# One 512-column output projection for two token blocks of a first MLP, in place of two of 256 columns

## The chip, the core and the metric

The kernel runs on one core of a Trainium2 chip. The metric is the device time of one execution in microseconds (us); of the kernel before there are three runs. The core has a matrix engine (TensorE, PE in the rows; its weight loads are PEld), a vector engine (VectorE, DVE), an engine for functions (ScalarE, ACT), a general one (GpSimd, POOL) and one that issues transfers (SyncE, SP). Each runs its own instruction stream in order, and semaphores hold it back until the data it needs are there. TensorE writes its sums into PSUM, which has eight banks of 512 float32 numbers per partition; all else lies in SBUF.

## What is computed

```python
def reference(q, k, v, moe_*, moe2_*):
    # 4 sequences, 8 heads, 576 tokens, head size 64; causal window of 64 keys
    scores = where(0 <= i - j < 64, q @ k.T / 8, -1e9)
    attn = softmax(scores) @ v
    x = attn.transpose(0, 2, 1, 3).reshape(2304, 512)
    x = (sigmoid(x @ w_gate) * (x @ w_val)) @ w_out      # 512 -> 1536 -> 512
    return ((x @ w_a) * (x @ w_b)) @ w_out2              # 512 -> 1536 -> 512
```

The weights reach the core as 64-bit floats, so each matrix is decoded on the chip to float32 and split into a pair (h, l) of float32r tiles that sum to it. Data are split likewise, and a product is three matmuls: h·h, h·l, l·h.

## The kernel before

The 2304 tokens are nine blocks of 256 (`N`). `HALVES` puts blocks 0 to 4 into a first half and 5 to 8 into a second; in each half blocks are grouped: (0), (1, 2), (3, 4), then (5, 6), (7, 8). A half runs the first MLP (phase 0) for its blocks and then the second (phase 1). The hidden dimension is 12 chunks of 128; a *turn* of the plan takes one group and one to three chunks. In a first MLP the turns with the first three chunks take one block each; all later turns of a two-block group take both blocks at once.

For each chunk of a turn `hidden` makes two products over the model dimension (`gps` and `vps`, lines 301 and 303, 12 matmuls each on line 293, 512 columns for two blocks and 256 for one), each in one PSUM bank of `ps_gv` (three banks). ScalarE and VectorE make of them the hidden pair `hh`, `hl` (lines 307 to 318), from a pool of five. The output projection of a turn isn't made at once: each block's job goes into `queue` and is put out in the next turn, spread over that turn's chunks (line 479). A job `projection` takes two banks of `ps_acc` (which has two), runs over the turn's chunks, the four 128-row chunks of the output and the three products (line 332, 256 columns), and then `evacuate` adds both banks to the block's sums `xacc` in SBUF (line 351 on VectorE; line 349 on ScalarE for a block's first turn). After a block's last chunk the sums are rounded to `xh` (line 356, ScalarE) and the rest goes to `xl` (line 357, GpSimd): the input of the second MLP.

Between the products, `decode` prepares the weights, one matrix at a time: ScalarE (line 259), VectorE (262, 266, 269), GpSimd (272), VectorE (274, the float step), ScalarE (279, the rounding to `wah`, `wbh` or `woh`) and GpSimd (280, the rest `wal`, `wbl`, `wol`). There are four places for a chunk's weights, so a chunk waits for the readers of the chunk four before it. What `tile` schedules as each engine's order is fixed when the program is built.

Of the kernel before, what the change touches and what calls it, by code (L numbers as in the profile page):

```python
# [19 lines left out]
def tile_window_attention_gated_mlps(ctx, tc, q, k, v, w1g, w1v, w1o, w2a, w2b, w2o, out):  # L20
# [5 lines left out]
    NP = H // 2            # head pairs = chunks of the model dimension  # L26
    NF = DFF // P          # chunks of the hidden dimension
    G = 3                  # hidden chunks whose products are summed in PSUM
    N = 256                # tokens of a block
    TB = N // P            # 128-token tiles of a block  # L30
    # blocks that share their products over the model dimension, in two halves
    HALVES = (((0,), (1, 2), (3, 4)), ((5, 6), (7, 8)))
    W = 2 * N
    LAG = 1                # steps between the starts of two units of attention
    WIN = 64
    KW = P + WIN           # keys that a 128-query tile can see
    QSCALE = -1.0 / float(D) ** 0.5    # scores are kept negated
# [20 lines left out]
    # the tensor engine's clock is up by the time that the first rows are here  # L58
# [3 lines left out]
    # queries in halves of 64, each with its window of 128 keys; the rows are those of two heads.  # L62
    # key c of the window, WIN - c tokens before the half's first query, is open to query p for
    # p + 1 <= c <= p + WIN
# [13 lines left out]
    # the first half of a sequence has no keys before it  # L78
# [3 lines left out]
    # ---------------------------------------------------------------- attention  # L82
# [3 lines left out]
    # columns: pair of heads, half of the queries, head of the pair, query; Q of the even heads  # L86
    # above zeros, of the odd heads below zeros
# [13 lines left out]
    def attention(t, hq, xhi, xlo, c0):  # L101
        """Tokens [128 t, 128 t + 128) of heads [4 hq, 4 hq + 4); the result, split, goes to columns
        c0... of xhi, xlo. A generator: it stops where other work may come between."""
# [9 lines left out]
        # keys' window of the transposed K, two heads to a column; scores are kept negated  # L113
        # the first units have the banks to themselves
# [18 lines left out]
        # V of the 64 keys before the tile and of its first half  # L133
# [57 lines left out]
    # places of x: the result of the first MLP follows its input, and each group of the second  # L191
    # half one of the first half
# [3 lines left out]
    def new_x(phase, group):  # L196
        """Tiles for x of a group, in parts that sum to it; blocks have their slices."""
        w = len(group) * N
        place = PLACE[group]
        x[phase, group] = pair = tuple(  # L200
            xs.tile([P, NP, w], F32R, tag=f"x{p}{place}", name=f"x{p}{phase}_{group[0]}") for p in "hl"
        )
        for i, b in enumerate(group):
            x[phase, (b,)] = tuple(t[:, :, i * N:(i + 1) * N] for t in pair)

# [9 lines left out]
    def attention_stream(blocks):  # L215
        """The units of the blocks, a new one under way every LAG steps."""
# [15 lines left out]
    # ------------------------------------------------------------------ weights  # L232
    mats = ((w1g, w1v, w1o), (w2a, w2b, w2o))
    words = [[w.bitcast(I32) for w in m] for m in mats]    # float64: low word, high word
# [16 lines left out]
    def decode(F):  # L251
        """Hidden chunk's weights: float64 words to float32 (rounded at the 24th bit) and on to
        float32r pairs that sum to it exactly. A generator, one matrix at a time."""
        got = {}
        for nm in "abo":
# [4 lines left out]
            # the exponent: what lies below float32's range becomes 0  # L260
# [24 lines left out]
    # --------------------------------------------------------------------- MLPs  # L285
    def product(ps, w, x):
        """ps = w^T x over the model dimension; the product of the two rests is below what the
        sums keep."""
# [9 lines left out]
    def hidden(phase, w, x):  # L298
# [6 lines left out]
        if phase == 0:  # L305
            # the logistic function is (1 + tanh(x / 2)) / 2; tanh is in one table set with exp
# [14 lines left out]
    def project(phase, acc, w, h, begin, end):  # L321
# [7 lines left out]
        for m, ps in enumerate(outs):  # L329
            for n, (a, b) in enumerate(pairs):  # L330
                # a start clears the written bits of the whole bank: one for both of its sums
# [8 lines left out]
    def evacuate(phase, blk, acc, begin, end):  # L340
        """Adds the products of a few hidden chunks to what the block has so far."""
# [20 lines left out]
    # The turns of a phase: a block and the hidden chunks it takes. They are staggered, so that  # L362
    # chunks are done with, and others are needed, one at a time.
    # the first turns, and before each what is to be ready: blocks of attention, chunks of weights
# [9 lines left out]
    def turns(order, half, ph):  # L374
# [11 lines left out]
        if (half, ph) == (0, 0):     # as blocks come in one by one  # L386
# [29 lines left out]
    def step_decode(turn):  # L416
        """One matrix of the next chunk, if the place for it is free in this turn."""
# [24 lines left out]
    def attend(blk=None, steps=0):  # L442
        """Puts out attention up to the end of a block, or so many steps of it."""
# [5 lines left out]
    def projection(ph, blk, work, begin, end):  # L449
# [3 lines left out]
        evacuate(ph, blk, acc, begin, end)  # L453

    queue, begun = [], 0
    for n, (half, ph, group, fcs) in enumerate(plan):
# [14 lines left out]
        for i, fc in enumerate(fcs):  # L471
# [3 lines left out]
            if (half, ph) == (0, 1) and fc == NF - 1 and PLACE[group] == PLACE[HALVES[1][1]]:  # L475
                # the last reader of this place's x is out
                attend(HALVES[1][0][-1])
                feed = attention_stream(HALVES[1][1])
            for _ in range(-(-len(queue) // (len(fcs) - i))):
                projection(*queue.pop(0))  # L480
            for _ in group:
                step_decode(n)
                attend(steps=rate)
        for j, b in enumerate(group):
            sl = slice(j * N, (j + 1) * N)
            queue.append((ph, b, [(w, (hh[:, sl], hl[:, sl])) for w, (hh, hl) in hs], begin, end))
# [32 lines left out]
```

## Time and profile before

| | |
|---|---|
| median of three runs | 1041.39 us (1040.54 to 1041.55) |
| span of the profiled execution (its own time isn't listed beside it) | 1039.7 us |
| TensorE busy | 1007.7 us, 97% |
| VectorE, ScalarE, GpSimd busy | 74%, 45%, 43% |
| DMA engines, mean share | 32% |

Busy time counts a matmul from its start to its end, and matmuls overlap; what one costs is read from the distance of the starts. A wait is put down to what the profile saw end last, which need not be what the instruction waited for. "Granted clock" is the share of TensorE's full clock that it was given: 1.00 is 2.4 GHz, 0.50 is 1.2 GHz.

### The profile page before, as it was taken

The numbers are of one execution on the slowest core, as the hardware profiler recorded it, in microseconds if no ns is written. First come the engines' busy times: TensorE is split into PE (matmuls) and PEld (weight loads), VectorE is DVE, ScalarE is ACT, GpSimd is POOL, SyncE is SP. The second block draws the span as 40 slices with busy tenths as digits, with TensorE's granted clock in tenths as the row PEclk, the third lists the DMA queues.
The fourth block names the chain that finished last, engine by engine and source line by source line (L and its number), as shares of the span: only waits on it lengthen the run. The fifth ranks groups of instructions, "written<-read, shape, count | busy, mean of one in ns | idle before, by whom it ended". The sixth has DMA issues, their size and how long they took to land.

```text
span 1039.7 us, 16966 instructions
## 1 busy us (share of the span) xinstructions
PE 1007.7 (97%) x6278; PEld 886.0 (85%) x6278; DVE 766.4 (74%) x1414; ACT 467.7 (45%) x1075; POOL 447.9 (43%) x353
## 2 busy tenths in 40 slices
PE   7799999999999999999999999999999799999998
PEld 6799998989899788888888898988888788888886
DVE  5998378767868956856767696468787877787853
ACT  7887543332334665433423566333333444333320
POOL 2554055434527713524434242245454675454520
PEclk9999999999999999999999999999999999999999
DMA  8866233212312323323312372123232323232302
GB/s 203 202 174 159 57 112 102 82 61 81 102 45 78 97 76 102 102 61 102 102 61 81 100 215 63 42 81 99 84 102 81 102 74 103 86 103 82 102 1 81
DMA packets 122930, 99.92 MB, mean 96 GB/s; under 512 B 60896, under 2 KB 114400, under 8 KB 122848
## 3 DMA queue, kind: packets, MB, share of 16 engines
q1 hardware_dynamic: 122848, 98.85, 32.4%
q8 instruction: 49, 0.80, 0.3%
q14 instruction: 33, 0.27, 0.1%
HBM read 89.65 MB, written 4.72 MB: 91 GB/s over the span
## 4 chain that ended last, share of the span: by engine, by line
PE 63%; DVE 19%; POOL 7%; ACT 6%; issue 4%; DMA 1%; SPq 0%; DVEq 0%; POOLq 0%; ACTq 0%
PE acc L332 20%; PE vps L293 19%; PE gps L293 19%; DVE ex L262 5%; DVE ex L274 3%; DVE wi L269 3%; DVE xacc L351 2%; POOL wi L272 2%; POOL wal L280 2%; PE sps L146 2%; DVE hl L316 2%; POOL wol L280 1%; POOL wbl L280 1%; PE xps L182 1%; DVE wi L266 1%
## 5 line engine op out<-in xcount | busy, mean ns | idle before, releaser
L272 POOL TENSOR_TENSOR wi<-wi,low 128x512 int32<-128x512 int32 x144 | 196.6, 1365 | 107.1 <-DVE wi L269 84.0
L293 PE MATMUL gps<-xh,wah 128*128 128x512 f32 (+1 forms) x528 | 188.3, 357 | 1.9 <-ACT wah L279 1.9
L293 PE MATMUL vps<-xh,wbh 128*128 128x512 f32 (+1 forms) x528 | 186.0, 352 | 1.7 <-ACT hr L307 0.9
L293 PE MATMUL gps<-xh,wal 128*128 128x512 f32 (+1 forms) x528 | 186.0, 352 | 0.0
L293 PE MATMUL gps<-xl,wah 128*128 128x512 f32 (+1 forms) x528 | 186.0, 352 | 0.0
L293 PE MATMUL vps<-xh,wbl 128*128 128x512 f32 (+1 forms) x528 | 185.7, 352 | 0.0
L293 PE MATMUL vps<-xl,wbh 128*128 128x512 f32 (+1 forms) x528 | 185.3, 351 | 0.0
L280 POOL TENSOR_TENSOR wol<-ex,woh 128x512 fp32r<-128x512 f32 x48 | 67.1, 1397 | 179.9 <-ACT woh L279 179.9
L315 ACT ACTIVATE hh<-hr 128x512 fp32r<-128x512 f32 (+1 forms) x132 | 73.0, 553 | 150.6 <-DVE hr L311 77.4
L280 POOL TENSOR_TENSOR wal<-ex,wah 128x512 fp32r<-128x512 f32 x48 | 71.5, 1490 | 143.8 <-ACT wah L279 126.1
L332 PE MATMUL acc<-hh,woh 128*128 128x256 f32 x432 | 123.6, 287 | 5.5 <-ACT woh L279 5.3
L332 PE MATMUL acc<-hl,woh 128*128 128x256 f32 x432 | 123.7, 287 | 0.6 <-DVE hl L316 0.6
L332 PE MATMUL acc<-hh,wol 128*128 128x256 f32 x432 | 123.4, 286 | 0.0
L274 DVE SCALAR_TENSOR_TENSOR ex<-ex,wi 128x512 f32<-128x512 int32 x144 | 102.8, 714 | 16.2 <-POOL wi L272 11.2
L293 PEld LDWEIGHTS vps<-xh,wbh 128*128 128x128 f32 x528 | 100.0, 189 | 15.7 <-ACT hr L307 1.3
L280 POOL TENSOR_TENSOR wbl<-ex,wbh 128x512 fp32r<-128x512 f32 x48 | 73.0, 1520 | 92.3 <-ACT wbh L279 89.0
L293 PEld LDWEIGHTS gps<-xh,wah 128*128 128x128 f32 x528 | 100.2, 190 | 14.5 <-ACT wah L279 2.0
L293 PEld LDWEIGHTS gps<-xh,wal 128*128 128x128 f32 x528 | 100.0, 189 | 13.7
L293 PEld LDWEIGHTS vps<-xh,wbl 128*128 128x128 f32 x528 | 99.8, 189 | 13.3
L293 PEld LDWEIGHTS vps<-xl,wbh 128*128 128x128 f32 x528 | 99.8, 189 | 13.2
L293 PEld LDWEIGHTS gps<-xl,wah 128*128 128x128 f32 x528 | 100.1, 190 | 12.1
L351 DVE TENSOR_TENSOR xacc<-acc,xacc 128x512 f32<-128x512 f32 x130 | 87.3, 683 | 26.8 <-PE acc L332 26.7
(76 smaller groups left out, 2000.0 us busy)
## 6 DMA issues: line engine op xcount, KB each, us to landing
st_o<-in_moe_w_out_dram SPq DMA_DIRECT2D x48, 512.0 KB, 3.6
st_a<-in_moe_w_gate_dram SPq DMA_DIRECT2D x24, 512.0 KB, 3.6
st_b<-in_moe_w_val_dram SPq DMA_DIRECT2D x24, 512.0 KB, 3.6
st_a<-in_moe_w_a_dram SPq DMA_DIRECT2D x24, 512.0 KB, 3.5
st_b<-in_moe_w_b_dram SPq DMA_DIRECT2D x24, 512.0 KB, 3.6
out_dram<-xacc SPq DMA_DIRECT2D x18, 256.0 KB, 2.0
vb<-v SPq DMA_DIRECT2D x68, 64.0 KB, 3.1
k<-in_k_dram SPq DMA_DIRECT2D x32, 128.0 KB, 3.2
```

The source lines that it names most:

```text
L146: nc.tensor.matmul(sps[:, s, j, :], lhsT=qt[:, j, s], rhs=kt[:, j, s * WIN:s * WIN + P], start=True, stop=True)
L182: nc.tensor.matmul(xps[rows, i // 2, s * WIN:(s + 1) * WIN], lhsT=vv[:, i, :], rhs=pt[:, s, i, :], start=True, stop=True)
L262: nc.vector.tensor_scalar(out=ex, in0=w1, scalar1=(1 << 31) - 1, scalar2=20, op0=ALU.bitwise_and, op1=ALU.logical_shift_right)
L269: nc.vector.scalar_tensor_tensor(out=wi, in0=w1, scalar=-(1 << 30), in1=wi, op0=ALU.bitwise_and, op1=ALU.bitwise_or)
L272: nc.gpsimd.tensor_tensor(out=wi, in0=wi, in1=low, op=ALU.add)
L274: nc.vector.scalar_tensor_tensor(out=wf, in0=ex, scalar=897.0, in1=wi.bitcast(F32), op0=ALU.is_ge, op1=ALU.mult)
L280: nc.gpsimd.tensor_tensor(out=wl, in0=wf, in1=wh.bitcast(F32), op=ALU.subtract)
L293: nc.tensor.matmul(ps, lhsT=a[:, c * P:(c + 1) * P], rhs=b[:, c, :], start=(n == 0), stop=(n == 3 * NP - 1))
L315: nc.scalar.activation(out=hh, in_=hr, func=AF.Copy, scale=factor)
L316: nc.vector.scalar_tensor_tensor(out=hl, in0=hr, scalar=factor, in1=hh.bitcast(F32), op0=ALU.mult, op1=ALU.subtract)
L332: nc.tensor.matmul(ps, lhsT=a[:, m * P:(m + 1) * P], rhs=b, start=begin and n == 0 and (phase == 1 or m % 2 == 0), stop=end and n == 2 and ...
L351: nc.vector.tensor_tensor(out=dst, in0=ps, in1=dst, op=ALU.add)
```

## The change

Turns of two blocks in a first MLP no longer queue one job for each block. They queue four jobs, one for each 128-row chunk `m` of the output: the stationary weights `oh` and `ol` of that chunk, with the hidden pairs of both blocks, 512 columns, as the moving operand, into one bank. Each bank is then added to the sums of its two blocks in two halves of 256 columns, and after the second and the fourth job the finished half of a block's sums is turned into the second MLP's input. Turns of one block and all of the second MLP stay as they were.

```diff
+    def wide_projection(group, work, m, begin, end):
...
+        ps = ps_acc.tile([P, 2, N], F32, tag="acc", name="accw")
+        flat = ps.rearrange("p b n -> p (b n)")
+        n, last = 0, 3 * len(work) - 1
+        for w, (hh, hl) in work:
+            oh, ol = w["o"]
+            for a, b in ((oh, hh), (oh, hl), (ol, hh)):
+                nc.tensor.matmul(flat, lhsT=a[:, m * P:(m + 1) * P], rhs=b, start=n == 0, stop=n == last)
+                n += 1
+        for i, b in enumerate(group):
+            dst = xacc[b][:, m // 2, m % 2, :]
+            if begin:
+                nc.scalar.activation(out=dst, in_=ps[:, i, :], func=AF.Copy)
+            else:
+                nc.vector.tensor_tensor(out=dst, in0=ps[:, i, :], in1=dst, op=ALU.add)
+        if end and m % 2 == 1:
+            for b in group:
+                xh, xl = (t[:, m - 1:m + 1, :] for t in x[1, (b,)])
+                dst = xacc[b][:, m // 2]
+                nc.scalar.activation(out=xh, in_=dst, func=AF.Copy)
+                nc.gpsimd.tensor_tensor(out=xl, in0=dst, in1=xh.bitcast(F32), op=ALU.subtract)
...
             for _ in range(-(-len(queue) // (len(fcs) - i))):
-                projection(*queue.pop(0))
+                job = queue.pop(0)
+                job[0](*job[1:])
...
+        if ph == 0 and len(group) == 2:
+            queue.extend((wide_projection, group, hs, m, begin, end) for m in range(NP))
+            continue
         for j, b in enumerate(group):
             sl = slice(j * N, (j + 1) * N)
-            queue.append((ph, b, [(w, (hh[:, sl], hl[:, sl])) for w, (hh, hl) in hs], begin, end))
+            queue.append((projection, ph, b, [(w, (hh[:, sl], hl[:, sl])) for w, (hh, hl) in hs], begin, end))
```

The orders below are those of the built programs. First TensorE in a steady turn of the second half's first MLP, before: a job's second output chunk and the start of its third, in the banks `acc0` and `acc1` (moving `hh` or `hl`, stationary `woh` or `wol`; the size is that of the output).

```order
L332 MATMUL acc0_8733<-hh_8479,woh_8289 128x256
L332 MATMUL acc0_8733<-hl_8480,woh_8289 128x256
L332 MATMUL acc0_8733<-hh_8479,wol_8290 128x256
L332 MATMUL acc1_8734<-hh_8479,woh_8289 128x256
L332 MATMUL acc1_8734<-hl_8480,woh_8289 128x256
L332 MATMUL acc1_8734<-hh_8479,wol_8290 128x256
```

The same engine and stage now, one whole job (`accw`) and the next hidden product.

```order
L469 MATMUL accw_8549<-hh_8251,woh_8077 128x512
L469 MATMUL accw_8549<-hl_8252,woh_8077 128x512
L469 MATMUL accw_8549<-hh_8251,wol_8078 128x512
L469 MATMUL accw_8549<-hh_8334,woh_8212 128x512
L469 MATMUL accw_8549<-hl_8335,woh_8212 128x512
L469 MATMUL accw_8549<-hh_8334,wol_8213 128x512
L469 MATMUL accw_8549<-hh_8398,woh_8359 128x512
L469 MATMUL accw_8549<-hl_8399,woh_8359 128x512
L469 MATMUL accw_8549<-hh_8398,wol_8360 128x512
L293 MATMUL gps_8587<-xh0_5_4088,wah_8423 128x512
```

A job of three chunks was 36 matmuls over two banks, chunk by chunk; it is 9 in one bank, all three chunks of one output chunk together, and reads the weights of all three chunks to its end.

Next ScalarE in the same stage, before, where the output weights `woh` of a new chunk wait for a free place (TensorE reads the old ones).

```order
L315 ACTIVATE hh_8578<-hr_8575 128x512 [waits DVE_49]
L279 ACTIVATE woh_8631<-ex_8624 128x512 [waits PE_49]
L279 ACTIVATE wah_8683<-ex_8676 128x512 [waits DVE_49]
L307 ACTIVATE hr_8667<-gps_8641 128x512 [waits PE_49,Activation_49]
L259 ACTIVATE low_8773<-st_o_8639 128x512 [waits DMAHW3_49,Activation_49,Pool_49]
```

And now:

```order
L307 ACTIVATE hr_8395<-gps_8369 128x512 [waits PE_49]
L279 ACTIVATE woh_8359<-ex_8352 128x512 [waits PE_49]
L315 ACTIVATE hh_8398<-hr_8395 128x512 [waits DVE_49,PE_49]
L279 ACTIVATE wah_8423<-ex_8416 128x512 [waits DVE_49]
L307 ACTIVATE hr_8466<-gps_8440 128x512 [waits PE_49,Activation_49]
```

The rounding of `woh` stood behind the hidden pair's `hh` and stands ahead of it now, and that `hh` has a wait for TensorE that it did not have.

Last VectorE where the second half's first MLP ends, before: the additions of block 8's last job.

```order
L308 SCALAR_TENSOR_TENSOR hr_9317<-hr_9317,vps_9304 128x512
L262 TENSOR_SCALAR ex_9495<-st_o_9289 128x512
L316 SCALAR_TENSOR_TENSOR hl_9321<-hr_9317,hh_9320 128x512
L274 SCALAR_TENSOR_TENSOR ex_9495<-ex_9495,wi_9497 128x512
L351 TENSOR_TENSOR xacc8_7957<-acc0_9324,xacc8_7957 128x512
L266 TENSOR_SCALAR wi_9560<-st_a_9506 128x512
L351 TENSOR_TENSOR xacc8_7957<-acc1_9325,xacc8_7957 128x512
```

And now, the additions of the third and fourth job of blocks 7 and 8:

```order
L308 SCALAR_TENSOR_TENSOR hr_8977<-hr_8977,vps_8964 128x512
L262 TENSOR_SCALAR ex_9014<-st_a_8945 128x512
L316 SCALAR_TENSOR_TENSOR hl_8981<-hr_8977,hh_8980 128x512
L274 SCALAR_TENSOR_TENSOR ex_9014<-ex_9014,wi_9016 128x512
L476 TENSOR_TENSOR xacc7_7629<-accw_8984,xacc7_7629 128x256
L476 TENSOR_TENSOR xacc8_7769<-accw_8984,xacc8_7769 128x256
L266 TENSOR_SCALAR wi_9029<-st_b_8947 128x512
L269 SCALAR_TENSOR_TENSOR wi_9029<-st_b_8947,wi_9029 128x512
L476 TENSOR_TENSOR xacc7_7629<-accw_8996,xacc7_7629 128x256
L476 TENSOR_TENSOR xacc8_7769<-accw_8996,xacc8_7769 128x256
L262 TENSOR_SCALAR ex_9027<-st_b_8947 128x512
L274 SCALAR_TENSOR_TENSOR ex_9027<-ex_9027,wi_9029 128x512
```

The additions still stand behind a decode step (line 274), of an earlier matrix than before (`st_a` instead of `st_o`); there are twice as many, of half the size, with two decode steps between the banks.

## Rows read from the trace of the kernel before

**Rows 1.** The page's busy times: engine, us, share of the span, instructions.
```profile
PE 1007.7 (97%) x6278; PEld 886.0 (85%) x6278; DVE 766.4 (74%) x1414; ACT 467.7 (45%) x1075; POOL 447.9 (43%) x353
```
**Rows 2.** Busy time by stretch (us from the start); columns as in the first line.
```profile
core 0: us, PE busy (x) PEld busy (x) DVE busy (x) ACT busy (x) POOL busy (x), PEclk, DMA share, GB/s
120.00:340.00 220.00, 219.19 (x1435) 200.38 (x1431) 162.09 (x230) 81.55 (x147) 100.59 (x74) 1.00 0.26 82
660.00:850.00 190.00, 183.85 (x1074) 163.93 (x1074) 146.81 (x200) 72.04 (x121) 99.35 (x71) 0.98 0.27 86
850.00:1039.70 189.70, 185.32 (x813) 151.83 (x811) 134.26 (x184) 64.56 (x109) 78.40 (x56) 1.00 0.25 81
```
**Rows 3.** The chain of waits, 222 to 232 us: start, us, engine, tile, line.
```profile
222.42 4.31 PE acc L332 x36
226.73 2.75 PE gps L293 x12
229.48 2.72 PE vps L293 x12
```
**Rows 4.** Groups by line and shape: busy us, mean ns | idle before, releasers.
```profile
L332 PE MATMUL acc<-hl,woh 128*128 128x256 f32 x432 | 123.7, 287 | 0.6 <-DVE hl L316 0.6
L351 DVE TENSOR_TENSOR xacc<-acc,xacc 128x512 f32<-128x512 f32 x130 | 87.3, 683 | 26.8 <-PE acc L332 26.7
L311 DVE TENSOR_TENSOR hr<-vps,hr 128x256 f32<-128x256 f32 x12 | 5.0, 417 | 7.1 <-PE vps L293 5.8 <-ACT hr L310 1.3
```
**Rows 5.** Timeline, chain and stretches around 824 us (start, us, engine, line).
```profile
822.06 1.77 DVE L274 SCALAR_TENSOR_TENSOR ex<-ex,wi 128x512 f32<-128x512 int32 x1 [1.18 <-POOL wi L272]
827.58 0.68 DVE L316 SCALAR_TENSOR_TENSOR hl<-hr,hh 128x512 fp32r<-128x512 f32 x1
828.78 0.68 DVE L351 TENSOR_TENSOR xacc<-acc,xacc 128x512 f32<-128x512 f32 x1
829.61 0.55 PE L332 MATMUL acc<-hh,woh 128*128 128x256 f32 x1 [5.29 <-ACT woh L279]
...
829.61 2.90 PE acc L332 x12
832.50 0.43 PE gps L293
833.36 3.86 PE acc L332 x24
...
830.00:835.00 5.00, 5.00 (x23) 4.81 (x23) 3.51 (x4) 1.99 (x4) 5.00 (x4) 0.50 0.28 98
```
**Rows 6.** Waits of TensorE: us in total, times, longest.
```profile
PE acc L332 <- ACT woh L279: 5.3, 1, 5.3
PE acc L332 <- DVE xacc L351: 1.8, 3, 1.4
PE acc L332 <- ACT xacc L349: 1.1, 1, 1.1
PE vps L293 <- ACT hr L307: 0.9, 1, 0.9
```
**Rows 7.** Decode in the second half: timeline rows, then pieces of the chain.
```profile
740.35 0.69 DVE L274 SCALAR_TENSOR_TENSOR ex<-ex,wi 128x512 f32<-128x512 int32 x1 [1.18 <-POOL wi L272]
744.85 0.28 PE L332 MATMUL acc<-hh,woh 128*128 128x256 f32 x1
746.93 0.61 ACT L279 ACTIVATE woh<-ex 128x512 fp32r<-128x512 f32 x1
787.46 1.78 POOL L280 TENSOR_TENSOR wbl<-ex,wbh 128x512 fp32r<-128x512 f32 x1 [2.71 <-ACT wbh L279]
801.91 0.39 PE L293 MATMUL vps<-xh,wbh 128*128 128x512 f32 x1
...
751.61 1.61 POOL wal L280
771.67 1.61 POOL wbl L280
```

## What I expect of the change

> **What bounds the kernel now.** I read the engines' busy times first, then the stages, then the starts of the matmuls, and last the waits. TensorE is busy for 97% of the span and no other engine for more than 74% [rows 1]. Such a share can hide gaps, since matmuls overlap, so the starts matter more. In the chain of waits 36 matmuls of 256 columns take 4.31 us and 12 of 512 columns 2.72 us, one group starting where the other ends [rows 3]: 119.7 ns from start to start for 256 columns, 226.7 ns for 512, with nothing between. By stages TensorE is idle for 0.8 of 220 us in the first half's first MLP, and for 6.2 of 190 us in the second half's (660 to 850) [rows 2]. All its waits on first-MLP sums come to some 9 us [rows 6]; 5.29 us of them are one wait, at 824 us [rows 5]. So a shorter instruction stream on TensorE shows in the time, unless something else comes late in its place.
>
> **Fewer matmuls.** Of 1296 matmuls of 256 columns in the output projections (3 groups of 432 [rows 4]), those of turns of two blocks change: each of the four groups of two blocks takes 9 of its 12 hidden chunks in such turns, so 4 groups x 9 chunks x 2 blocks x 12 = 864. They become 432 of 512 columns. One of 512 for two of 256 saves 2 x 119.7 - 226.7 = 12.7 ns, and 432 x 12.7 ns = **5.5 us**. The 226.7 ns is of the same form: float32r, 128 x 512, one full bank as output. The other end is no gain (2 x 119.7 ns); more isn't to be had, as no row shows 512 columns faster. Weight loads halve too, but they lie beside the matmuls (a distance of 119.7 ns holds a load and a matmul), and I count nothing for them.
>
> The Trainium skill ("TensorE: Matmul & The Clock Gate", "Wait — 56ns, not 53.3ns?") gives a warm matmul its columns over 2.4 GHz plus about 2.5 ns. By that the merge would be worth an estimated 432 x 2.5 ns = 1.1 us. The rows disagree: 119.7 and 226.7 ns are each some 13 ns above the columns' time at the granted clock of 1.00, so the measured intervals decide and the rule is left as a small rival.
>
> **More evictions.** There are 14 such turns. Each had 4 additions of 128x512 at 683 ns on VectorE; now 8 of 128x256. The nearest row is line 311 at 128x256, also an addition-like operation of a PSUM and an SBUF operand: 417 ns [rows 4]. That is 112 x 417 - 56 x 683 ns = 8.5 us more for VectorE (0.6 us a turn; ends: 0 if half the size took half the time, 38 us if it took the full 683 ns). VectorE is 74% busy and the evictions lie under the next chunk's hidden product, 24 x 226.7 ns = 5.4 us. So nothing on the path as long as they aren't queued behind a decode step. Per bank the cover improves: a job now fills one bank, in 9 x 226.7 ns = 2.0 us, and the next job but one reuses it. The conversions to the second MLP's input (lines 356 and 357) keep number and size. No DMA changes in number.
>
> **Later release of weights and of the hidden pair.** A turn of three chunks used to put the two waiting jobs behind its first and second chunk; four jobs now go 2, 1, 1, so the last reads its weights behind the third chunk. The slot of the output weights is released one hidden product and two-thirds of a job later, about 5.4 + 1.3 = 6.7 us. The decoder waits there: chunk 8's last float step ends at 741.0 us and its rounding to woh starts only at 746.9, when the matmuls from 744.85 on are through with the old slot [rows 7]. Decode has about 6 us of slack in a cycle of three chunks, and this slack isn't eaten, since the cycle repeats: the release moves once against TensorE. What shrinks is the lead of decoded weights. In the tightest case the last wbl is made from 787.46 to 789.24 us and first used at 801.91 [rows 7], so 12.7 us become about 6. I cost it at nothing; the cover is those 6 us. The third chunk's hidden pair now waits for the last job as well (ScalarE's order), under 1 us, with 2.0 + 2.9 us until it is needed.
>
> **The end of the second half's first MLP.** At 824 us TensorE waits 5.29 us. The waits' list names woh, but what the next job needs is an accumulator bank, and VectorE starts that eviction at 828.78, ends it at 829.46, 0.15 us before the matmul [rows 5]. It stood behind decode steps (one at 822.06, 1.77 us long, after a wait for GpSimd) and line 316 at 827.58. Then the granted clock is 0.50 (1.2 GHz) from 830 to 835 [rows 5]: 12 matmuls take 2.90 us for 1.44, two of 512 columns 0.43 for 0.23 each, 24 take 3.86 for 2.87 [rows 5], together 2.9 us. The place costs 5.3 + 2.9 = 8.2 us.
>
> After the change TensorE's order there runs: two jobs of blocks 7 and 8, twelve hidden matmuls on the half of the input that is ready, two jobs of blocks 5 and 6, and so on. The banks of the last two jobs must be free 2.7 us after these end. From the last weight release (t = 0), TensorE ends them at 1.4 + 2 x 5.4 + 4.1 + 4.1 = 20.4 and wants the banks at 23.1. The decode step ahead of the evictions is the fourth matrix after the release; the first one's float step comes about 3 us after its release (woh is made at 746.93, the next matrix's rest at 751.61 [rows 7], two short steps behind its float step) and each further one about 5 later (751.61 and 771.67 are four matrices apart [rows 7]), so 18, plus two rests of the new input on GpSimd, some 1.6 us each like those of the weights [rows 7]: 21. Four evictions and a decode step end at 23.5 to 25; rounding (2 x 0.6, as woh [rows 7]) and rests (2 x 1.6) for the second half of the input end near 28 to 29, where TensorE wants it at 26.3. I expect 2 to 5 us of waits in pieces, perhaps with some slow clock, for 8.2 us. Ends: all 8.2 gone, and as bad as before. I take **3 us** back, and count the waits at 340 to 355 us (1.4 and 1.1 us [rows 6]) as unchanged, since their evictions stay behind the same kind of steps.
>
> **Sum.** 5.5 + 3 = 8.5 us off the span of 1039.7 us gives 1031.2; the median of the runs lies 1.7 us above that span, so **1033 us**.
>
> **Rivals.**
> - *The end of the MLP gains nothing* (the wait takes other forms): 1041.4 - 5.5 = 1035.9. For it: VectorE's order keeps decode steps ahead of evictions. Chance 0.20.
> - *It vanishes*: 1041.4 - 5.5 - 8.2 = 1027.7. Against it: the float step at t = 21. 0.10.
> - *Decode becomes the bound in the second half.* The chain there runs through decode for long stretches [rows 7], and with TensorE faster its lead is thinner. Then the second half's share, 216 x 12.7 ns = 2.7 us, is waited away and the MLP's end stays: 1041.4 - 2.8 = 1038.6. Against it: the lead of 6 us. 0.12.
> - *The merge saves only the small fixed part*, 1.1 us: 1040.3. Against it: the rows' 12.7 ns. 0.03. *It does nothing at all* (512 columns into the shared bank at 2 x 119.7 ns): 1041.4. 0.04.
> - *Slower*: a bank not evicted in time in a turn of two blocks, because VectorE holds the additions of the first two jobs behind a decode step of the second weight matrix; in the second half's steady turns that is the eighth float step after the release, 3 + 7 x 5.0 = 38 us, and the first bank is free at 39 or 40, while the third job comes 1.4 + 5 x 5.4 + 4.1 + 2.0 + 2.0 + 4.1 = 40.6 us after it. A wait long enough to lower the clock costs what the place at 824 us costs, 8.2 us; one such wait more than now gives 1041.4 - 5.5 + 8.2 = 1044.1, two 1052. It decides from 5.5 us of new waits on, 0.4 us a turn over 14 turns. Against it: apart from the starts of phases, no wait of TensorE for VectorE or ScalarE is above 0.9 us now [rows 6]. 0.09.
>
> The Trainium skill speaks for this last one ("TensorE: Matmul & The Clock Gate", "A second HAM failure mode: psum-queue depth-cycling"): a kernel that cycles through PSUM banks can idle TensorE often enough to lose its clock between bursts. The trace agrees on the fall after a wait (0.50 behind the 5.29 us), but shows 1.00 in the second MLP, where jobs cycle through two banks too [rows 2].
>
> **How the numbers follow.** The forecast has 0.42, the rivals 0.20, 0.10, 0.12, 0.03, 0.04 and 0.09. From 1027.5 to 1039.5 us lie the forecast, its two neighbours and decode as the bound, 0.84, less a little at both edges. This kernel's measurement can tell about 0.2%, 2.1 us, from no change. Faster by more: 0.42 + 0.20 + 0.10 + three-quarters of 0.12 = 0.81. Within: the rest of 0.12, and 0.07: 0.10. Slower: 0.09.
>
> **What would show it.** Right: matmuls of the new line start 226.7 ns apart, 9 in 2.0 us; 432 fewer matmuls; near 820 us less idle time of TensorE than 5.3 us and a granted clock near 1.00; woh waits for TensorE grow without TensorE waiting for weights. Wrong: starts further apart than 227 ns; TensorE waiting for additions in many turns; hidden products waiting for wah or wbh; a stretch at 0.50 that was at 1.00.

## The result: slower, 1051.1 against 1041.0 us

| | before | after |
|---|---|---|
| median of four runs | 1041.03 us (1040.54 to 1041.55) | 1051.12 us (1049.64 to 1052.30) |
| ratio, 95% interval | | 1.0094 (1.0079 to 1.0108) |
| span of the profiled execution | 1039.7 us | 1048.0 us |

The changed kernel is 0.9% slower; 1033.0 us was predicted. The page's busy times of the changed kernel, the counterpart of [rows 1]:

```profile
PE 1005.5 (96%) x5846; PEld 859.3 (82%) x5846; DVE 781.4 (75%) x1470; ACT 466.0 (44%) x1075; POOL 445.8 (43%) x353
```

TensorE has 432 matmuls fewer, as it should, and VectorE 15 us more work. Groups by line and shape (busy us, mean ns of one | idle before), for [rows 4]:

```profile
L469 PE MATMUL accw<-hh,woh 128*128 128x512 f32 x144 | 57.1, 398 | 7.2 <-DVE xacc L476 5.7 <-DVE xacc L351 1.5
L469 PE MATMUL accw<-hl,woh 128*128 128x512 f32 x144 | 56.5, 392 | 2.4 <-DVE hl L316 2.4
L476 DVE TENSOR_TENSOR xacc<-accw,xacc 128x256 f32<-128x256 f32 x112 | 41.1, 412 | 0.7 <-PE accw L469 0.7
L351 DVE TENSOR_TENSOR xacc<-acc,xacc 128x512 f32<-128x512 f32 x74 | 49.9, 685 | 18.9 <-PE acc L332 18.9
```

The chain of waits shows a job without a gap, for [rows 3] (start, us, tile, count):

```profile
724.14 2.04 PE accw L469 x9
726.18 2.72 PE gps L293 x12
728.90 2.72 PE vps L293 x12
```

Nine in 2.04 us are 226.7 ns apart. The saving is there, then, and waits ate it. TensorE's waits in the changed kernel (total, times, longest), for [rows 6]:

```profile
PE accw L469 <- DVE xacc L476: 5.7, 6, 1.9
PE gps L293 <- POOL xl L482: 3.3, 2, 1.7
PE acc L332 <- DVE xacc L351: 2.6, 4, 1.7
PE vps L293 <- ACT hr L310: 2.4, 3, 1.0
PE accw L469 <- DVE hl L316: 2.4, 3, 1.5
```

No wait is as long as the 5.3 us of [rows 6]; there are many, most of 0.5 to 1.9 us. Not one of these is for a weight: they are for additions, hidden rows and the second MLP's input. (One wait of 0.5 us for a weight, at 52 us, stands in both kernels.) Adding up what the distances between matmul starts hold beyond the usual one of their shape gives 66.8 us for the changed kernel and 52.9 us for the kernel before; 13.9 us more, less the 5.5 us saved, is about the 8.3 us between the spans.

**Where it is lost.** Both programs start the same 3168 hidden products (line 293) in the same order, so the n-th of one can be set against the n-th of the other. The table gives how far TensorE falls behind the kernel before (a minus: gains) in each stage, in us; times are those of the kernel before. What differs before 144 us is left out. The edges lie where all kernels have put out the same jobs. The stages are the first half's first MLP (from its first two-block turns), its end and the start of the second MLP, the rest of that, the second half's first MLP, its end, and its second MLP. The kernels below the first line are those of the experiments.

| kernel | 144–314 | 314–411 | 411–669 | 669–789 | 789–873 | 873–end |
|---|---|---|---|---|---|---|
| changed kernel | +1.7 | +4.0 | 0.0 | −2.5 | −1.0 | +5.9 |
| a_pairs | −2.6 | 0.0 | 0.0 | +1.3 | −2.0 | +2.2 |
| b_late | +3.0 | +3.9 | 0.0 | −1.2 | +0.7 | +1.2 |
| a_oneadd | +0.7 | +3.4 | 0.0 | −2.9 | −2.1 | +4.8 |
| a_both | −2.6 | −0.6 | 0.0 | +0.7 | 0.0 | +0.2 |
| a_early | −2.6 | −1.7 | 0.0 | +2.0 | −0.4 | 0.0 |
| a_shave | +3.9 | +5.8 | 0.0 | −2.5 | −0.6 | +6.0 |
| a_wo5 | +3.8 | +2.9 | −1.7 | +5.1 | −1.0 | +5.3 |
| a_hp6 | +2.5 | +5.8 | 0.0 | −2.6 | −0.8 | +5.9 |
| a_olate | +2.4 | +3.1 | −1.8 | +5.1 | −1.0 | +5.2 |
| a_endpairs | +1.7 | +4.0 | 0.0 | −2.5 | −0.9 | +5.9 |
| a_midpairs | −2.6 | +0.1 | 0.0 | +1.2 | −2.0 | +2.2 |

The matmuls alone, 12.7 ns for each of the 432 wide ones, should give −2.4, −0.4, 0.0, −1.8, −1.0 and 0.0 in the six columns (186, 30, 0, 138, 78 and 0 of them). The rest of the changed kernel's row are waits: +4.1 and +4.4 us in the first two columns, then 0.0, −0.8, 0.0 and +5.9. In a_pairs the first column has hardly any new wait, and there the saving shows (−2.6).

The expectations of a_endpairs and a_midpairs below name 4.0 and 1.4 us for a_pairs. They were read with an edge at 312 us, where a_pairs is between two jobs; their sum is the same as here.

**What is late.** ScalarE around chunk 7's output weights, in the changed kernel (start, us, line, what it waited for):

```profile
190.54 0.42 ACT L315 ACTIVATE hh<-hr 128x256 fp32r<-128x256 f32 x1 [0.60 <-DVE hr L308]
193.57 0.39 ACT L307 ACTIVATE hr<-gps 128x256 f32<-128x256 f32 x1 [2.62 <-PE gps L293]
195.42 0.63 ACT L279 ACTIVATE woh<-ex 128x512 fp32r<-128x512 f32 x1 [1.46 <-PE accw L469]
195.96 0.40 ACT L315 ACTIVATE hh<-hr 128x256 fp32r<-128x256 f32 x1
199.46 0.64 ACT L279 ACTIVATE wah<-ex 128x512 fp32r<-128x512 f32 x1 [3.10 <-DVE ex L274]
```

And in the kernel before:

```profile
189.63 0.42 ACT L315 ACTIVATE hh<-hr 128x256 fp32r<-128x256 f32 x1 [0.61 <-DVE hr L308]
190.43 0.63 ACT L279 ACTIVATE woh<-ex 128x512 fp32r<-128x512 f32 x1 [0.38 <-PE acc L332]
194.12 0.63 ACT L279 ACTIVATE wah<-ex 128x512 fp32r<-128x512 f32 x1 [3.07 <-DVE ex L274]
```

The place for `woh` is free when the last job has read it, and that job now stands behind the third chunk: 195.42 against 190.43, 5.0 us later, where the prediction reckoned with 6.7. The next `wah` moves with it, since the decode has one place for its float word `ex`. At chunk 31 the same happens once more. Its `woh`, first in the kernel before, then in the changed kernel:

```profile
725.92 0.63 ACT L279 ACTIVATE woh<-ex 128x512 fp32r<-128x512 f32 x1 [0.47 <-PE gps L293]
...
735.53 0.62 ACT L279 ACTIVATE woh<-ex 128x512 fp32r<-128x512 f32 x1
```

That is 9.6 us later, of which 5.2 us were there already at chunk 30 and 4.4 are new. By the starts of these `woh` operations, decoded weights are level with the kernel before up to chunk 6 (0.1 us), 5.0 us behind at chunk 7 and 5.8 through the first half's second MLP, with 6 to 9 in between. They are 9.6 behind at chunk 31, up to 14 behind in the second half's first MLP, and 8.3 from chunk 42 to the last; 8.3 us is also what TensorE ends behind. Decode waits for places that TensorE frees, so this alone does not say which of the two holds up the other.

### The profile page after: what moved, and what is told of

Read it like the earlier page. It is cut to its first block, busy times and chain, and to the rows that moved or that the text cites. A ratio compares the mean times of both kernels' runs of the same rounds, so it can differ in the third digit from the quotient of the medians.

```text
span 1048.0 us, 16217 instructions
## 1 busy us (share of the span) xinstructions
PE 1005.5 (96%) x5846; PEld 859.3 (82%) x5846; DVE 781.4 (75%) x1470; ACT 466.0 (44%) x1075; POOL 445.8 (43%) x353
## 4 chain that ended last, share of the span: by engine, by line
PE 58%; DVE 24%; POOL 6%; ACT 6%; issue 4%; DMA 1%; DVEq 0%; POOLq 0%; SPq 0%; ACTq 0%
PE vps L293 18%; PE gps L293 18%; PE acc L332 12%; DVE ex L262 6%; PE accw L469 5%; DVE wi L269 5%; DVE ex L274 3%; DVE hl L316 3%; DVE wi L266 2%; PE sps L146 2%; POOL wi L272 2%; DVE xacc L476 2%; POOL wol L280 1%; POOL wbl L280 1%; POOL wal L280 1%
## 5 line engine op out<-in xcount | busy, mean ns | idle before, releaser
L316 DVE SCALAR_TENSOR_TENSOR hl<-hr,hh 128x512 fp32r<-128x512 f32 (+1 forms) x132 | 91.6, 694 | 40.1 <-ACT hh L315 39.3
L274 DVE SCALAR_TENSOR_TENSOR ex<-ex,wi 128x512 f32<-128x512 int32 x144 | 106.8, 741 | 16.9 <-POOL wi L272 11.5
L332 PE MATMUL acc<-woh,hh 128*128 128x512 f32 x216 | 85.0, 393 | 4.5 <-DVE xacc L351 2.6
L332 PE MATMUL acc<-woh,hl 128*128 128x512 f32 x216 | 84.0, 390 | 0.5 <-DVE hl L316 0.5
L332 PE MATMUL acc<-wol,hh 128*128 128x512 f32 x216 | 84.3, 390 | 0.0
```

What stands on the lines that cost most here:

```text
L274: nc.vector.scalar_tensor_tensor(out=wf, in0=ex, scalar=897.0, in1=wi.bitcast(F32), op0=ALU.is_ge, op1=ALU.mult)
L316: nc.vector.scalar_tensor_tensor(out=hl, in0=hr, scalar=factor, in1=hh.bitcast(F32), op0=ALU.mult, op1=ALU.subtract)
L332: nc.tensor.matmul(ps, lhsT=a[:, m * P:(m + 1) * P], rhs=b, start=begin and n == 0 and (phase == 1 or m % 2 == 0), stop=end and n == 2 and ...
```

## The experiments

"Theory 1" holds the late last job for the cause; the names in the short diffs are those of the kernel. Each ratio is to the kernel before, with its 95% interval.

**The position, from both sides.** a_pairs keeps the wide matmuls but takes the four jobs in two pairs, so that the last stands behind the second chunk again.

```diff
-            queue.extend((wide_projection, group, hs, m, begin, end) for m in range(NP))
+            queue.extend((wide_pair, group, hs, m, begin, end) for m in range(0, NP, 2))
```

> The changed kernel with its four jobs of a two-block turn queued as two pairs (output chunks 0 and 1, then 2 and 3), so that the last reader of a chunk's output weights and hidden pair stands behind the second chunk of the next turn, as in the kernel before. Theory 1 (the later release of weights and hidden pairs pushes decode back against TensorE, and in-order engines then hold TensorE up): the loss goes, 1034 to 1039 us, and the second MLP of the second half shows no waits above 1 us. Theory 2 (twice as many additions of half the size keep VectorE behind): stays at 1047 to 1052 us.

1040.55 us, 0.9996 (0.9987 to 1.0006): 10.6 us better than the changed kernel, level with the kernel before, and so above the 1034 to 1039 us of theory 1 but far from theory 2's. The second half's second MLP still has one wait above 1 us (1.4). b_late is the opposite, the kernel before with nothing but the second of two waiting jobs put behind the third chunk.

```diff
-            for _ in range(-(-len(queue) // (len(fcs) - i))):
+            jobs = -(-len(queue) // (len(fcs) - i))
+            if queue and queue[0][0] == 0 and queue[0][5] and len(fcs) == 3:
+                jobs = (1, 0, 1)[i]
```

> The kernel before, with 256-column jobs, but where two jobs of a two-block turn of the first MLP meet a turn of three chunks, the second job stands behind the third chunk and not behind the second. Matmuls and additions are those of the kernel before. Theory 1 (later release): slower by about what the changed kernel loses beside its 5.5 us of saved matmuls, 8 to 15 us, so 1049 to 1056 us. Theory 2 (smaller additions): 1040 to 1043 us.

1049.89 us, 1.0079 (1.0064 to 1.0094): the loss without the wide matmuls. TensorE's waits for additions in its first half, from 144 to 315 us and from 312 to 412 us:

```profile
PE acc L332 <- DVE xacc L351: 2.2, 1, 2.2
...
PE acc L332 <- DVE xacc L351: 2.6, 2, 2.1
```

Position costs 8 to 11 us, most of it in the first half (first two columns of the table: +5.7 and +6.9 with the late job, −2.6 without).

**The smaller additions.** a_oneadd holds both blocks' sums in one tile and adds each bank with one 128x512 operation; the jobs stay late. a_both adds the pairs to it.

```diff
-        for i, b in enumerate(group):
-            dst = xacc[b][:, m // 2, m % 2, :]
...
+        sums = xpair[0, group][:, m // 2, m % 2, :]
+        nc.vector.tensor_tensor(out=sums, in0=flat, in1=sums, op=ALU.add)
```

> The changed kernel with the sums of two blocks in one tile, so that one addition of 128x512 takes a whole bank, as many and as large as in the kernel before; the jobs stand where the change puts them. Theory 1 (later release): stays at 1047 to 1052 us. Theory 2 (smaller additions): the loss goes, 1035 to 1040 us.

> Jobs in pairs and one addition for a bank together. Theory 1: as the pairs alone, 1033 to 1038 us. Theory 2: as the single addition alone, 1035 to 1040 us. If both count, faster than either, about 1033 us.

a_oneadd 1047.37 us, 1.0050 (1.0035 to 1.0065); a_both 1039.62 us, 0.9983 (0.9974 to 0.9993), above the 1033 us expected if both count. One addition for two gives 3.7 us with the late jobs, 0.9 us with the pairs. a_both is faster than either kernel, by 0.17% of the kernel before. In a_early (one addition, all four jobs behind the next turn's first chunk) the last reader is earlier still:

```diff
-            for _ in range(-(-len(queue) // (len(fcs) - i))):
+            wide = queue and queue[0][0] is wide_projection
+            for _ in range(len(queue) if wide else -(-len(queue) // (len(fcs) - i))):
```

> The single addition for a bank, and all four jobs of a two-block turn behind the first chunk of the next turn: the weights' places come free one hidden product and more earlier than in the kernel before. If the time of the release drives the time also in this direction: 1033 to 1038 us. Rival (four jobs in a row fill two banks faster than VectorE empties them between decode steps, and TensorE waits for additions): 1040 us or more, with waits of TensorE for the additions in most turns of two blocks.

1039.67 us, 0.9988 (0.9979 to 0.9997). Earlier than the second chunk gains nothing more in all: −4.2 in the first half's columns, +1.6 in the second half's.

**More places for what the late job holds.** a_shave makes room in SBUF (4 instead of 5 places for `kts` and `vs`, 2 of 3 for `vb`, 3 of 5 for `small`) and is the control; a_wo5 adds a fifth place for the output weights, a_hp6 a sixth for the hidden pair.

```diff
-            wh = wts.tile([P, DM], F32R, tag=f"w{nm}h", name=f"w{nm}h")
+            places = 5 if nm == "o" else G + 1
+            wh = wts.tile([P, DM], F32R, tag=f"w{nm}h", bufs=places, name=f"w{nm}h")
```

> A control for the next two: the changed kernel with fewer buffers in the attention (keys 4 for 5, values 4 for 5, the shifted values 2 for 3, small tiles 3 for 5), which makes room for one more place. All theories: the changed kernel's time, 1047 to 1054 us.

> The control with five places for a chunk's output weights instead of four, so that decode doesn't wait for the last job of the turn before. Theory 1a (of the two later releases it is that of the output weights, which pushes decode back): most of the loss goes, 1039 to 1044 us. Theory 1b (it is that of the hidden pair, which blocks ScalarE): as the control, 1047 to 1054 us.

> The control with six places for the hidden pair instead of five, so that the third chunk's hidden pair doesn't wait for the last job of the turn before. Theory 1a (output weights): as the control, 1047 to 1054 us. Theory 1b (hidden pair): most of the loss goes, 1039 to 1044 us.

1053.69 us, 1.0120 (1.0105 to 1.0135); 1055.97, 1.0142 (1.0127 to 1.0158); 1052.91, 1.0115 (1.0098 to 1.0132). Neither place cures it. With the fifth place the decode did run ahead: `woh` of chunks 7 to 15 starts 3.5 to 18 us before that of the kernel before, that of chunk 31 starts 2 us before it instead of 9.6 behind. Half of the loss at 314–411 went (5.8 to 2.9), but 144–314 stayed (3.9 to 3.8), and 669–789 turned from −2.5 to +5.1. So 144–314 loses as much with weights that are decoded early. The sixth place for the hidden pair had little to lift: ScalarE's idle time before line 315 is put down to VectorE alone in the control.

**The queue in ScalarE, the banks.** a_low2 gives the decode's first word `low` a second place, since ScalarE waits over 200 us in sum for the one place, with hidden rows behind it; a_acc3 gives `acc` a third bank, from attention.

```diff
-            low = dec.tile([P, DM], I32, tag="low", name="low")
+            low = dec.tile([P, DM], I32, tag="low", bufs=2, name="low")
```

```diff
-    ps_acc = ctx.enter_context(tc.tile_pool(name="ps_acc", bufs=2, space=PSUM))
+    ps_acc = ctx.enter_context(tc.tile_pool(name="ps_acc", bufs=3, space=PSUM))
```

> Changed kernel with a second place for the decode's word `low` (2 KB), paid for by 4 instead of 5 places for attention's keys and 3 instead of 5 for its small tiles. Today ScalarE waits 104 to 106 times, some 207 to 230 us in sum, for GpSimd to read the one `low` before it writes the next, and whatever stands behind it in ScalarE's order (the next hidden row L310, L307) waits too. Theory 3 (the late last job costs time because decode steps that run late relative to TensorE stand ahead of hidden rows and additions in the in-order queues of ScalarE and VectorE): most of the loss of the second half's second MLP (5.9 us) and some of the first half's goes, 1041 to 1047 us. Rival (VectorE or the banks hold TensorE, ScalarE's wait for `low` costs nothing): within 2 us of the changed kernel's 1051.1, or up to the 1053.7 of the kernel with attention's places shaved.

> The kernel before with the second place for `low` and the same shaved places: the control for a_low2. If the place helps whatever the position of the last job, it gains here as much as there (1034 to 1039 us); if it only undoes what the late job costs, within 2 us of 1041.

> The kernel of a_early (one addition for each bank, all four jobs behind the next turn's first chunk; 1039.7 us) with the second place for `low`. Theory 3: its remaining waits for hidden rows (hl, hr: 2.8 + 1.8 + 1.4 + 1.0 us) shrink, 1031 to 1037 us. Rival (the decode's total rate or VectorE's load sets the end of each MLP): 1038 to 1042 us.

> Changed kernel with three PSUM accumulators (`acc`) instead of two, the third taken from attention (2 instead of 3). Theory 2 (a new chunk of the output finds its bank not yet added up, since the four jobs follow in twos and the last stands shortly before the next turn's first): the waits for the additions L476 and L351 (5.7 + 2.6 + 1.8 + 1.5 us in the changed kernel) fall below 4 us and the time to 1041 to 1046 us. Rival (TensorE would wait a little later for the same VectorE and ScalarE queues, the waits only change their names): 1048 to 1053 us, with more for attention's lost place.

a_low2 1051.99 us, 1.0110 (1.0093 to 1.0127), b_low2 1042.41, 1.0014 (1.0005 to 1.0023), a_early_low2 1039.74, 0.9989 (0.9980 to 0.9998): the second place gains nothing anywhere. But it did not take the wait away that it was meant to. ScalarE's waits for `low`, in the changed kernel and in a_low2:

```profile
ACT low L259 <- POOL wi L272: 216.9, 102, 3.9
...
ACT low L259 <- POOL wi L272: 208.4, 101, 3.9
```

With two places, `low` is written one matrix earlier, again right after GpSimd has read what was in its place (0.03 us after, median), and ScalarE stands there as long as before. So theory 3 is not tested by these three kernels.

a_acc3 took 1062.84 us, 1.0211 (1.0196 to 1.0227); 10.5 us of that are lost before 144 us, where attention lacks its bank. From 144 to 411 us it loses 8.9 us, the changed kernel 5.7. In the second half, by the last hidden product, TensorE falls behind by 1.9 us with three banks and by 2.4 with two. Its waits changed names: in a_acc3 as a whole they read

```profile
PE vps L293 <- ACT hr L310: 7.6, 5, 2.2
...
PE accw L469 <- DVE xacc L476: 3.6, 3, 2.4
PE accw L469 <- DVE hl L316: 2.8, 3, 1.5
```

so a third bank does not take the loss away, and theory 2 in this form falls.

**The stop of the decode.** The four next kernels decode each chunk's output weights one chunk later, so that their place should be free when they come.

```diff
+    def unit(U):
+        return [(nm, F) for nm, F in (("a", U), ("b", U), ("o", U - 1)) if 0 <= F < NW]
...
-        for nm in "abo":
-            st = staged.pop((F, nm))
+        for nm, f in unit(F):
+            st = staged.pop((f, nm))
```

> Changed kernel with each chunk's output weights (woh, wol) loaded and decoded one chunk later, behind the next chunk's two other matrices; the queue of jobs, the additions and the places stay as they are. In the changed kernel the decode stands still where woh of chunks 7 and 31 waits for the last, late job to read its place (ready at 184.8 and 729.1 us, written at 195.4 and 735.5 us; in the kernel before 190.4 and 725.9 us); from there on every later chunk is 5 and 4.4 us later than before. Theory 4 (this stop, with all of the decode that stands behind it in order, is what the late job costs): with the output weights a chunk later their place is free when they come, the stops of chunks 7 and 31 go, and the time falls by 5 to 10 us to 1041 to 1046 us. Rival (the stop only moves, to the next matrix or to TensorE, which then waits for the later woh): 1049 us or more.

> The kernel before with the output weights decoded one chunk later, the control: its own stops at woh of chunks 7, 9 and 32 (190.4, 233.6, 746.9 us) should go as well. Theory 4: a gain, but less than in the changed kernel, 1034 to 1040 us. Rival: within 2 us of 1041, or slower where TensorE waits for the later woh.

> One addition for each bank (a_oneadd, 1047.4 us) with the output weights decoded one chunk later: the jobs stay late (2, 1, 1). Theory 4: both causes of the loss are gone, so the 5.5 us of the wider matmuls show at last: 1033 to 1040 us. Rival: 1044 us or more.

> a_early (all four jobs behind the next turn's first chunk, one addition for each bank; 1039.7 us) with the output weights decoded one chunk later. Theory 4: with the jobs early little of the stop is left to take away, 1034 to 1040 us, and no more than 3 us below a_oneadd_olate. Rival (the position costs by something else than the stop): at least 4 us below a_oneadd_olate.

1053.62 us, 1.0118 (1.0103 to 1.0133); 1048.83, 1.0073 (1.0056 to 1.0090); 1050.24, 1.0085 (1.0070 to 1.0100); 1046.76, 1.0053 (1.0038 to 1.0068). All are slower than what they were made from, and theory 4's times fall. (a_early_olate is 3.5 us below a_oneadd_olate, between the two limits that were set.) The edit has a price of its own, 7 to 8 us where jobs are early (b_olate, a_early_olate) and 2.5 to 3 where they are late; the position still costs 4.8 us (a_olate over b_olate) of 10.1. TensorE in a_olate, at a place where the changed kernel has no wait:

```profile
748.81 0.39 PE L297 MATMUL vps<-xh,wbl 128*128 128x512 f32 x1
751.56 0.47 PE L473 MATMUL accw<-hh,woh 128*128 128x512 f32 x1 [2.37 <-DVE xacc L480]
```

and VectorE beside it (lines 480, 320, 272 and 265 are 476, 316, 269 and 262 of the changed kernel):

```profile
748.40 0.68 DVE L320 SCALAR_TENSOR_TENSOR hl<-hr,hh 128x512 fp32r<-128x512 f32 x1
749.00 1.75 DVE L272 SCALAR_TENSOR_TENSOR wi<-st_o,wi 128x512 int32<-128x512 int32 x1
750.67 0.74 DVE L480 TENSOR_TENSOR xacc<-accw,xacc 128x256 f32<-128x256 f32 x2
```

The addition that frees the bank stands behind a decode step, by the fixed order of VectorE. By the last hidden product ahead of that job, decode has begun 101 matrices in a_olate and 99 in the changed kernel. Here, then, decode that runs ahead does not help a TensorE that waits for what is queued behind it.

**Which turns.** The last two undo the late position in some turns only: a_endpairs in each group's last turn of the first MLP, whose additions make the second MLP's input; a_midpairs in all others.

```diff
+            if end:
+                queue.extend((wide_pair, group, hs, m, begin, end) for m in range(0, NP, 2))
+            else:
+                queue.extend((wide_projection, group, hs, m, begin, end) for m in range(NP))
```

> Changed kernel with the four jobs in two pairs, as in a_pairs (1040.6 us), but only for the last turn of a group in the first MLP; its other turns keep the last job behind the third chunk. By stage, against the kernel before, the changed kernel loses 1.8 us from 144 to 312 us (a_pairs gains 4.0 there), 4.0 us from 312 to 411 us, the end of the first half's first MLP (a_pairs loses 1.4), and 2.4 us in the whole second half (a_pairs 1.5). Theory 5 (two separate costs in the first half: within the MLP the late job stops the decode, and at its end the additions of the late last job hold up the conversion of the second MLP's input): 144 to 312 stays at +1.8, 312 to 411 falls to about +1.4, the total 1047 to 1049 us. Rival (one cost: the decode, late since its stop at chunk 7, is what TensorE meets at the MLP's end): 312 to 411 stays at about +4, 1050 us or more.

> The other half of a_pairs: pairs in all turns of the first MLP but a group's last. Theory 5: 144 to 312 gains about 4 us as in a_pairs, 312 to 411 loses 4 as in the changed kernel, the total 1043 to 1046 us. Rival (one cost): nearly all of it comes back, 1042 us or less. In the second half neither kernel should stand more than 2.5 us from the kernel before: five orders of the jobs differ there by 2.6 us only.

a_endpairs 1050.44 us, 1.0089 (1.0069 to 1.0108); a_midpairs 1041.12, 0.9999 (0.9990 to 1.0009). The two rows of the table are, to 0.1 us, those of the changed kernel and of a_pairs. TensorE's longer waits from 312 to 412 us, in a_endpairs:

```profile
PE accw L469 <- DVE xacc L476: 2.0, 1, 2.0
PE acc L332 <- DVE xacc L476: 1.6, 1, 1.6
PE accw L469 <- DVE xacc L351: 1.5, 2, 0.8
PE gps L293 <- POOL xl L357: 1.2, 1, 1.2
```

and in a_midpairs, where the last turns are as late as in the changed kernel:

```profile
PE acc L332 <- DVE xacc L476: 2.3, 1, 2.3
PE sps L146 <- ACT qt L128: 1.6, 1, 1.6
```

So the 4 us lost at the MLP's end are not made there. They are what the turns before have left, and the late job of the last turn costs nothing: theory 5 falls, and both times that its rival of one cost named came. The rival takes what is left over for the late decode. That is not shown: in a_wo5 decode was early, and 314–411 still lost 2.9 us.

**What is settled and what is open.** Shown: the late last job of the first MLP's middle turns carries the whole loss against the kernel before (a_midpairs, a_endpairs), without the wide matmuls too (b_late), and mostly in the first half; halving the additions costs 3.7 us as long as jobs are late. The 5.5 us of the matmuls do not come back with the position: a_pairs has 4.2 us of new waits in the second half, 3.0 of them at 669–789. Not settled is how much of the loss each of the coupled waits carries. The decode's stop at chunks 7 and 31 is in the trace, but lifting it (a_wo5, a_olate) let other waits grow. Each edit of that kind also let the scheduler put the decode steps at other places in the engines' orders. A kernel with the stop lifted and the order kept was not tried, nor one in which ScalarE's wait for `low` goes. Open too is why in the second half five positions of the jobs (changed kernel, a_pairs, b_late, a_both, a_early) all end 0.7 to 2.4 us behind the kernel before, whether they gain or lose in its first MLP.

## Why the prediction was wrong

- **Fewer matmuls, −5.5 us: right.** 226.7 ns from start to start, 432 fewer. In a_pairs, where the first column has hardly a new wait, 2.6 us show for the 2.4 that its 186 wide matmuls should give. The small fixed part that the Trainium skill ("TensorE: Matmul & The Clock Gate", "Wait — 56ns, not 53.3ns?") would have left, an estimated 1.1 us, is not what these rows show.
- **More evictions, "nothing on the path": the size right, the cover wrong.** 412 ns each, against 417; but the additions did stand behind decode steps, the condition that the text named and then passed over. They cost 3.7 us by a_oneadd, as long as the jobs are late. (Of VectorE's 15 us more, 8 are additions; the rest lies in operations that are as many as before, such as line 316, 7 us more in sum.)
- **Later release, "I cost it at nothing; the cover is those 6 us": the step that failed.** The release moved by 5.0 us in the first half and by 4.4 in the second, once in each, and decoded weights got later by that, as reasoned. The cover held as it was worded: no new wait of TensorE is for a weight. But the lead of weights was the wrong cover. VectorE and ScalarE each run in one order that holds the decode, the hidden rows and the additions. TensorE waited for hidden rows and additions, and where rows are shown here these stand behind decode steps, which now ran 5 to 14 us later while TensorE itself was 0 to 8 us behind. The price of the moved job was 8.5 us (b_late) to 10.6 us (a_pairs against the changed kernel). The price and its source, the position, are shown; that it is paid by way of these orders is read from rows, and no run isolates it. The chain in [rows 7] hinted at it: from 749 to 829 us it runs through decode steps, hidden rows and additions, with no use of the weights by TensorE between them.
- **The end of the second half's first MLP, −3 us: nothing came.** The row's −1.0 at 789–873 is that of its 78 wide matmuls. By the distances between starts, waits and slow clock took 8.3 us there before, and waits in pieces take 8.3 us now, as the first rival had it (0.20). Waits from 800 to 865 us in the changed kernel, of which those at line 293 are for the second MLP's input:

```profile
PE gps L293 <- POOL xl L482: 3.3, 2, 1.7
PE accw L469 <- DVE xacc L476: 2.2, 3, 1.1
```

- **The waits at 340 to 355 us "as unchanged": wrong.** 314–411 lost 4.0 us, 4.4 in waits. VectorE and TensorE there in the changed kernel:

```profile
335.32 1.19 DVE L266 TENSOR_SCALAR wi<-st_o 128x512 int32<-128x512 int32 x1
336.43 0.68 DVE L351 TENSOR_TENSOR xacc<-acc,xacc 128x512 f32<-128x512 f32 x1
...
337.17 0.50 PE L469 MATMUL accw<-hh,woh 128*128 128x512 f32 x1 [0.68 <-DVE xacc L351]
```

  The addition behind the decode step again. By a_endpairs and a_midpairs this was a consequence of the middle turns, which the prediction, stage by stage, could not see.
- **The rivals.** The slower one named the form that most of the new waits took (a bank not emptied in time, its additions behind a decode step) and the right point to decide, 5.5 us of new waits; there were 13.9. But it sought one or two waits long enough to lower the clock. What came were many short ones at full clock: the granted clock of 820 to 865 us is 1.00, where [rows 5] have 0.50.

```profile
820.00:865.00 45.00, 39.19 (x164) 29.84 (x163) 39.78 (x52) 19.68 (x35) 31.52 (x23) 1.00 0.27 82
```

  Its evidence against, that hardly any wait was above 0.9 us now, spoke of an order in which the last job stood a chunk earlier. The rival of a bound in the second half gave away the 2.7 us gained there, and that much came: the second half gains nothing over the kernel before in any position of the jobs. Whether by its mechanism, decode as the bound, is not shown, and it had no eye for the first half.

## What to carry to other kernels

When an edit moves the last reader of a buffer, don't stop at the buffer's next user: ask which in-order queues its refill stands in, and what else is queued behind it there. Then see in the trace that an edit made to lift a wait has lifted it, before its time is held against a theory. Split jobs can be put back to where the last reader was by popping them in groups, which here was worth 10 us against the 5.5 us of the edit itself. Comparing the n-th instruction of two traces, stage by stage, showed where time is lost better than the lists of waits did, provided that both programs have done the same work at the edges of a stage. Two complementary half-edits tell a cause from its consequence.

## What the runs showed of the hardware

The decode's integer steps on VectorE have two durations. VectorE and GpSimd in the changed kernel (start, us, line):

```profile
887.16 0.42 DVE L266 TENSOR_SCALAR wi<-st_o 128x512 int32<-128x512 int32 x1
887.62 1.67 DVE L269 SCALAR_TENSOR_TENSOR wi<-st_o,wi 128x512 int32<-128x512 int32 x1
889.81 1.51 DVE L262 TENSOR_SCALAR ex<-st_o 128x512 int32<-128x512 int32 x1
...
887.39 1.34 POOL L280 TENSOR_TENSOR wbl<-ex,wbh 128x512 fp32r<-128x512 f32 x1 [1.82 <-ACT wbh L279]
889.43 1.60 POOL L272 TENSOR_TENSOR wi<-wi,low 128x512 int32<-128x512 int32 x1 [0.69 <-DVE wi L269]
```

In the kernel before, line 262 takes 0.41 to 0.43 us in its 25 runs with GpSimd idle, and 1.36 us on average in the 103 that lie beside a GpSimd operation for more than half their time; line 351, which reads PSUM, takes 0.68 us in both cases. The Trainium skill ("SBUF — State Buffer") calls the pair of ports that the two engines share exclusive, held for a whole instruction ("Terms"). The rows agree, with about 1 us for each such meeting of line 262. So a decode step in front of an addition can cost more than its own 0.4 us.
